# Moving weight loads in a fused attention and gated-FFN kernel: two gate/up pieces ahead of two stores, the down weights' loads retied, 40 instead of 64 rows in an opening load

## The chip, the cores and the metric

The kernel runs on one core of a Trainium2 chip. The metric is the device time of one execution in microseconds (us); lower is better. The core has TensorE (PE in the profile; its weight loads are PEld), VectorE (DVE), ScalarE (ACT), GpSimd (POOL) and SyncE (SP), which run in parallel and wait for each other by semaphores. [...]

## The reference

One transformer layer over x of 2048 rows by 640, in bf16. First a layer norm, then attention in 64 segments of 32 rows with a recurrent memory of 8 rows, then a residual, a second layer norm and a gated FFN, and a residual again.

```python
def _A_ref(x, mem0, Wq, Wk, Wv, Wo, seg_len):     # 32 heads of 128
    mem = mem0
    for s in range(n_seg):                         # 64 segments of 32 rows
        h = concat([mem, x[:, 32*s:32*s+32]])      # 40 rows
        q, k, v = h@Wq, h@Wk, h@Wv
        o = softmax(mask(q@k.T * Dh**-0.5)) @ v @ Wo
        mem = o[:, :8]                             # next segment's memory
        outs.append(o[:, 8:])

def _B_ref(x, W_gate, W_up, W_down):               # 640 -> 1728 -> 640
    return (relu(x @ W_gate) * (x @ W_up)) @ W_down

h  = x + _A_ref(_layernorm(x), ...)
h2 = h + _B_ref(_layernorm(h), ...)
```

A segment needs the memory that the segment before it made, so the 64 segments run one after the other.

## The kernel before

**How the order is made.** The program is a list of operations, each with an engine, the keys it reads and the keys it writes (`add`, `dma`, L348). `solve` (L46) puts a wait where a key was last written or read on another engine or by a DMA. Every engine executes its own operations in the order of the list. So the place of a `dma` call among the others decides its place in SP's queue, and nothing else: SP doesn't compute. While an SP operation waits, all that stands behind it on SP waits too.

**Opening (L746 to L793).** Nothing is in the chip's memory yet. SP issues the loads of Wk, Wq and Wv (15 loads of 1 MB) and of Wo (8 of 640 KB). ACT's queue loads 128 rows of x into `xt` (rows 0 to 63, then the last 64 rows of x), 128 rows into `x0` and the first memory. `row_stats`, `row_scale`, `ln1_trans` and `ln1_back` with b < 0 (L437 to L468) normalize and transpose `xt` and put it where the projections read it: the first 24 rows of each of segments 0 and 1 to `act_r`, the last 8 rows of segments 0, 1, 62 and 63 to `act_e`. Those last 8 rows are projected in groups of four segments. The first 24 rows of segments 62 and 63 aren't taken from this load.

**Segments (loop at L1026).** Each segment projects its rows, forms scores, probabilities, values and the output projection. Attention output rows go to a buffer in device memory, `attn_d`. The FFN is cut into four blocks of 512 rows, b = 0 to 3. As the attention ends, its weights' places are free one by one, and FFN weights are loaded into them: gate and up (Wg, Wu) where Wq was, down (Wd) where Wk was. The keys ("Wdone", j) say that all projections with Wq (0), Wk (1) or Wv (2) are through.

**FFN pieces.** The 1728 gate and up columns are 13 chunks j of 128 and a tail of 64. A pair is gate and up of one chunk (`gate_up`, L914): ten matmuls, a relu on ACT, a product on DVE into `hT`. Block 0's chunks 0 to 2 were computed during the last segments and come back from device memory into `hT` (the load from `hx_d`, L1300). Pair p of block 0 is chunk j = 3 + p. The pairs p = 0 to 3 run in the last segment's gaps; their matmuls have the line L832. From p = 4 on the line is L928, and the tail's is L941. Gate and up weights arrive in pieces (`load_piece`, L817), each with a key after which it may be issued: after the last VM load of segment 63, after the product of chunk NE (3), and so on. VM are copies of the attention values that `pv_x` (L692) reads.

**Down weights.** `load_down(n, p)` (L1260) loads chunks 3n to 3n + 2 of Wd, once Wk is free and the product of chunk 3 + p is there; n = 4 loads chunk 12 and the two halves of the tail. `down_pair` (L1235) multiplies; its first `down_part` (L1195) takes chunks 0 to 11 and so waits for Wd loads 0 to 3 at once. Its matmuls have the lines L1204 and L384.

**Rows and the second layer norm.** `rows` (L1270) projects the outputs of the last two segments: matmuls (L663), a copy on ACT and a sum on DVE (L1274) into `xt` or `xl`, then two stores of 24 rows to `attn_d`. For block 1, `ln2_load` (L731) loads x rows and attention rows, `ln2_front` (L736) adds them (L724) and normalizes on DVE and ACT, and `ln2_back` transposes them by DMA (L372). `h_rows` is block 0's residual, loaded from `h_d`; `down_out` (L1223, a DVE sum at L1226) adds it and `down_store` writes the result.

The order of SP's queue in the tail, as the list has it before the change: the VM loads, the two stores of segment 62's rows, two Wg pieces (chunks 7 to 10), a Wu piece, x and attention rows, a Wu piece, Wg and Wu for chunks 11 and 12, the load from hx, two stores of segment 63's rows, x and attention rows, two stores of late rows, four small loads of the gate/up tail (Wt), x and attention rows, Wd 0, x and attention rows, Wd 1, 2 and 3, h, Wd 4 with the tail, and the DMA transposes with the last gate and up pieces.

Of the kernel before, what the change touches and what calls it, by code (L numbers as in the profile page):

```python
# [177 lines left out]
def build_kernel(nc, A_x, A_mem0, A_Wq, A_Wk, A_Wv, A_Wo, A_seg_len, B_W_gate, B_W_up, B_W_down, out):  # L178
    _, S, D = A_x.shape
    M = A_mem0.shape[1]  # L180
    _, H, Dh = A_Wq.shape
    SEG = int(A_seg_len)
# [10 lines left out]
    RID = SEG - M  # L193
# [3 lines left out]
    x_ap, out_ap, mem0_ap = A_x[0], out[0], A_mem0[0]  # L197
# [4 lines left out]
    NE = 3  # L202
# [29 lines left out]
    hT = [ffn.alloc(f"hT{i}", [128, FC, TB], BF16) for i in range(2)]  # L232
# [6 lines left out]
    act_r = [ar.alloc(f"act_r{i}", [128, 4, DC, 32], BF16) for i in range(2)]  # L239
    act_e = [ar.alloc(f"act_e{i}", [128, DC, 32], BF16) for i in range(2)]  # L240
# [10 lines left out]
    VM = [ar.alloc(f"VM{i}", [128, 8, VW], BF16) for i in range(2)]  # L251
# [13 lines left out]
    xt = ar.alloc("xt", [128, D], BF16)  # L265
# [8 lines left out]
    def bank(b):  # L274
        return ps[:, b * 512:(b + 1) * 512]

    def bank_bf(b):
        return ps[:, b * 512:(b + 1) * 512].bitcast(BF16)
# [16 lines left out]
    def B(n):  # L295
        return ("B", n)
# [8 lines left out]
    for i in range(2):  # L305
        add("pool", lambda p, i=i: p.memset(act_r[i][:], 0.0),
            w=[("act", i, j, "m") for j in range(4)] + [("act", i, "x")] + [("act", i, "x", j) for j in range(4)])
# [6 lines left out]
    for g in range(4):  # L314
        for j in range(4):
            for r in range(2):
                sl, n = mca[32 * g:32 * g + 32, j, r, :], 0 if r == g % 2 else 1 + j
# [30 lines left out]
    def dma(dst, src, r=(), w=(), eng="sp"):  # L348
        add(eng, lambda e: e.dma_start(dst, src), r=r, w=w, dma=True)  # L349
# [12 lines left out]
    def row_stats(src, skey, n, more=()):  # L362
        row_moments(src, skey, n, more)
        row_std(n)

    def row_scale(src, skey, n, dst, dkey, eng="dve"):
        add(eng, lambda v: v.tensor_scalar(dst[0:n, :], src[0:n, :], mv[0:n, 0:1], rs[0:n, 0:1], ALU.subtract,
                                             ALU.mult), r=[skey, ("mv",), ("rs",)], w=[dkey])
# [5 lines left out]
    def transpose_rows(src, skey, n, b):  # L374
        def f(pe):
            for c in range(DC):
                i = pe.matmul(bank_bf(b)[:, c * 128:c * 128 + n], src[0:n, c * 128:(c + 1) * 128], ident[0:n, 0:n],
                              is_transpose=True)
            return i
        add("pe", f, r=[skey, ("ident",)], w=[B(b)])  # L380
# [56 lines left out]
            add("dve", lambda v: v.tensor_copy(dst, src), r=r, w=w)  # L437

    def n_rows(b):
        return 128 if b < 0 else min(128, S - 64 - 128 * b)  # L440

    def ln1_load(b, buf, key, eng="sp"):
        t0, n = 64 + 128 * b, n_rows(b)
        dma(buf[0:n, :], x_ap[t0:t0 + n, :], w=[key], eng=eng)

    def ln1_trans(b, buf, key, bk):
        transpose_rows(buf, key, 128 if b < 0 else min(128, S - 64 - 128 * b), bk)

    def ln1_back(b, src, r, eng):

        n = n_rows(b)

        def copy(dst, sl, w):
            if eng == "pool":
                add("pool", lambda p: p.tensor_copy(dst, sl), r=r, w=w)
            else:
                add("dve", lambda v: v.tensor_copy(dst, sl), r=r, w=w)
        if b < 0:
            for e in range(2):
                copy(act_r[1][:, e, :, M:32], src[:, :, SEG * e:SEG * e + RID], [("act", 1, "x", e)])  # L460
            copy(act_e[1][:, :, :].rearrange("p c (e t) -> p c e t", t=M),
                 src[:, :, :].rearrange("p c (e t) -> p c e t", t=SEG)[:, :, :, RID:SEG], [("acte", 1)])
            return
        for j in range(n // SEG):
            k = place(4 * b + 2 + j)[1]
            copy(act_r[b % 2][:, k, :, M:32], src[:, :, SEG * j:SEG * j + RID], [("act", b % 2, "x", k)])
        for j in range(n // SEG if n == 128 else 0):
            copy(act_e[b % 2][:, :, M * j:M * j + M], src[:, :, SEG * j + RID:SEG * j + SEG], [("acte", b % 2)])  # L468
# [277 lines left out]


    x0 = oTe[:].rearrange("p h t -> p (h t)")[:, 0:D]
    for n, t0 in enumerate((0, S - 64)):
        dma(xt[64 * n:64 * n + 64, :], x_ap[t0:t0 + 64, :], w=[("xt", "late") if n else ("xt",)], eng="act")  # L750
    ln1_load(0, x0, ("oTe", 0), "act")

    def mem_load(g, eng):
# [13 lines left out]
            A_Wo[16 * i + 4 * lo:16 * i + 4 * hi].rearrange("(g c) (p f) d -> (c p) g (f d)", c=4, f=4), w=[("Wo", i, lo)])  # L767
    ln1_load(1, xl, ("xl",))

    row_stats(xt, ("xt",), 128, [("xt", "late")])  # L770
    row_scale(xt, ("xt",), 128, xt, ("xt",))
    ln1_trans(-1, xt, ("xt",), P0)
    ln1_back(-1, chunks_of(bank_bf(P0)[:, 0:D]), [B(P0)], "dve")
    row_stats(x0, ("oTe", 0), 128)
# [13 lines left out]
    for j in (1, 0):  # L788
# [3 lines left out]
        for n, bks in enumerate(OB[j]):  # L792
            for i in range(2):  # L793
                t = 2 * (n % 2) + i
# [22 lines left out]
    def load_piece(key, eng="sp"):  # L817
        t, n, src, g, lo, hi = pieces.pop(0)
        a, b = GROUPS[g]
        dma(t[:, lo:hi, a:b], src[128 * lo:128 * hi, a:b].rearrange("(c p) f -> p c f", p=128), r=[("Wdone", 0), key],  # L820
            w=[(("Wg", "Wu")[n], g, lo)], eng=eng)
# [204 lines left out]
    for s in range(1, NSEG):  # L1026
# [16 lines left out]
        if s > 0:  # L1043
            a, ks = pass_act(s)
# [3 lines left out]
            elif s == NSEG - 3:  # L1048
                for n in range(2):
                    dma(ends[:, 1024 * n:1024 * n + 1024], ends_d[:, 1024 * n:1024 * n + 1024], r=[("ends",)],  # L1050
                        w=END_KEYS[2 * n:2 * n + 2])
# [32 lines left out]
            if s == NSEG - 2:  # L1084
                for n, (lo, hi) in enumerate(((0, 1), (1, 2), (2, 3), (3, DC))):
                    dma(xn2T[0][:, lo:hi, :], xn2_d[:, lo:hi, :], r=[("xn2_d", u) for u in range(4)] + [("Wdone", 0)],
                        w=[("xn2", 0, n)])
# [65 lines left out]
        if s == NSEG - 2:  # L1153
            p = 1 - place(s + 1)[0]
            add("pool", lambda o, p=p: o.tensor_copy(Qo[:, :, M:32], Qe[p][:, :, M:32]), r=[("Qe", p, i) for i in range(2)],
                w=[("Qo", i) for i in range(2)])
# [30 lines left out]
        if s == NSEG - 4:  # L1187
            p, j = place(NSEG - 1)
# [71 lines left out]
    def load_down(n, p):  # L1260
        lo, hi = 3 * n, min(3 * n + 3, FC - 1)
        r = [("Wdone", 1), ("hT", 0, NE + p)]
        dma(Wd[:, lo:hi, :], B_W_down[128 * lo:128 * hi, :].rearrange("(j p) d -> p j d", p=128), r=r, w=[("Wd", n)])
        if n == 4:
            for q in range(2):
                dma(Wd[FR * q:FR * q + FR, FC - 1, :], B_W_down[FM:F, :], r=r, w=[("Wd", 5 + q)])
# [3 lines left out]
    def rows(bk, p, s):  # L1270
        halves_pass(bk, oT[p], oT_keys(p, 0) + oT_keys(p, 1), range(16))
        tmp = bass.AP(at, 0, [[D, 64], [1, D]]).bitcast(F32)
        add("act", lambda a: a.activation(tmp, bank(bk)[64:128, 0:320], ACTF.Copy), r=[B(bk)], w=[("at",)])
        add("dve", lambda v: v.tensor_tensor(rowbuf(p), tmp,  # L1274
                                             bank(bk)[0:64, 0:320], ALU.add), r=[B(bk), ("at",)], w=[("wtok", p), (("xl",), ("xt",))[p]])
        for dg in range(2):
            dma(attn_d[32 * s:32 * s + RID, 2 * dg:2 * dg + 2, :].rearrange("t g f -> t (g f)"),
                bass.AP((xl, xt)[p], (32 * dg + M) * D, [[D, RID], [1, 320]]), r=[("wtok", p)],
                w=[("attn", 32 * s, g) for g in (2 * dg, 2 * dg + 1)])

    def rowbuf(p):
        return bass.AP((xl, xt)[p], 0, [[D, 64], [1, 320]])

    rows(P3, s % 2, s - 1)
    gate_up(0, NE + 1)
    load_piece(("VM", 0, 3))
    load_piece(("hT", 0, NE))
    pv_x(s, P0)
    norm_x(P0)
    norm_x_late(P0)  # L1290
# [8 lines left out]
    load_piece(("hT", 0, NE + 3))  # L1299
    dma(hT[0][:, 0:NE, :], hx_d[:, :, :], r=[("Wdone", 2), ("hT", 0, NE + 3)] + [("hx", n) for n in range(NE)],  # L1300
        w=[("hT", 0, n) for n in range(NE)])
    rows(P2, (s + 1) % 2, s)
    ln2_load(5)
    woe_pass(P3, range(16))
# [3 lines left out]
    for b in range(NBLK):  # L1308
        if 0 < b < NBLK - 1:
            for u in range(4):  # L1310
                ln2_load(4 * (b + 1) + u)
        for j in range(FC):
            p = j - NE if b == 0 else j
            if b or p > 3:
                gate_up(b, j)
            if b == 0 and p == 4:
                for q, src in enumerate((B_W_gate, B_W_up)):
                    for e in range(2):
                        r0 = FR * (q ^ e)
                        dma(Wt[:, e, :, r0:r0 + FR], src[:, FM:F].rearrange("(c p) f -> p c f", p=128),  # L1320
                            r=[("Wdone", 0), ("hT", 0, j)], w=[("Wt", q, e)])
            if b == 0 and p in (4, 5):
                ln2_load(p + 2)
            if b == 0 and 4 <= p < 8:
                for n in ((0,), (1, 2), (3,), (4,))[p - 4]:
                    load_down(n, p)
            if b == 0 and p == 6:
                dma(h_rows[0][:, :, :], h_d[:, :].rearrange("(u p) d -> p u d", p=128), r=[("h_d", u) for u in range(4)] +
                    [("Wdone", 1), ("hT", 0, j)], w=[("h", 0, u) for u in range(4)])
            if b == 0 and p in (8, 9):  # L1330
                load_piece(("hT", 0, j))
                load_piece(("hT", 0, j))
            if b + 1 < NBLK:
                fronts, backs = ((4, 6), (7, 9)) if b == 0 else ((1, 3, 5, 7), (3, 5, 7, 9))
                if p in fronts:
                    ln2_front(4 * (b + 1) + fronts.index(p))
                if p in backs:
                    ln2_back(4 * (b + 1) + backs.index(p), None)
        if b == 0:
            for u in (6, 7):  # L1340
                ln2_front(u)
                ln2_back(u, None)
        assert not pieces
        for n in range(2):
            down_pair(b, n)
# [63 lines left out]
```

## Time and profile before

| | |
|---|---|
| median of 3 runs | 998.86 us (998.84 to 999.37) |
| the profiled execution | 997.24 us |
| its span in the profile | 995.5 us |
| TensorE busy | 967.0 us (97%) |
| VectorE, ScalarE, GpSimd busy | 711.4, 521.4, 167.0 us |
| granted TensorE clock | 1.0 |
| opening, until the last Wv load is there | 0 to 41 us |
| tail of block 0 (from pair 0 to the end of its down projection) | 811 to 858.6 us |

The profile shows one execution of its own; its time is 997.24 us, 1.74 us more than its span, and 1.62 us less than the median of the runs shown. A busy TensorE isn't TensorE at its peak: matmuls are pipelined and their ends are modelled. The chain that ended last is followed back from the last instruction; what stands in it sets the end, and idle time of an engine outside it costs nothing. In a timeline row the first number is the start in us from the span's start, the second the duration, then engine, line, operation and tiles; the brackets say how long the engine stood idle before, and what released it. "SPq" is SP's queue: its rows say when a load was issued, not when it landed.

### The profile page before, as it was taken

What the parts mean: (1) busy time and instruction counts of PE and PEld (TensorE: products, weight loads), DVE (VectorE), ACT (ScalarE), POOL (GpSimd) and SP (SyncE); (2) the same over time, 40 slices, a digit from 0 to 9 for tenths busy, and PEclk for the clock granted to TensorE, in tenths of its full rate; (3) what the DMA queues carried; (4) which work ended last, traced back from release to release, by engine and by line L of the source; (5) the groups of instructions that cost most, each with busy time, mean ns of one, the idle gap of its engine ahead of it and who ended that gap; (6) DMA issues with size and microseconds to landing.
All of it is one profiled execution on the core that took longest, in us unless ns stands there. A gap on an engine that the chain in (4) does not pass through costs nothing.

```text
span 995.5 us, 56301 instructions
## 1 busy us (share of the span) xinstructions
PE 967.0 (97%) x26077; PEld 530.9 (53%) x24848; DVE 711.4 (71%) x1856; ACT 521.4 (52%) x1324; POOL 167.0 (17%) x412
## 2 busy tenths in 40 slices
PE   4799999999999999999999999999999999999998
PEld 1145555556555555555555655556565564444443
DVE  2468787878887887888788878787877865445332
ACT  1356666666666666666666666656665552122120
POOL 7011202021312130213022202021210010000000
PEclk9999999999999999999999999999999999999999
DMA  9941212121222122212312131112123259613100
GB/s 364 418 146 36 51 32 54 28 54 50 59 45 54 48 54 42 54 52 51 46 49 54 48 55 41 44 46 41 40 62 79 78 148 262 146 20 96 24 14 27
DMA packets 79135, 77.43 MB, mean 78 GB/s; under 512 B 45328, under 2 KB 64816, under 8 KB 76976
## 3 DMA queue, kind: packets, MB, share of 16 engines
q1 hardware_dynamic: 77136, 72.84, 26.6%
q8 instruction: 200, 3.28, 1.4%
q10 hardware_dynamic: 1760, 0.99, 0.4%
q14 instruction: 39, 0.32, 0.1%
HBM read 39.94 MB, written 7.74 MB: 48 GB/s over the span
## 4 chain that ended last, share of the span: by engine, by line
PE 93%; DMA 3%; DVE 1%; SPq 1%; issue 0%; ACT 0%; POOL 0%; DVEq 0%; ACTq 0%; POOLq 0%
PE ps L411 47%; PE ps L928 9%; PE ps L384 8%; PE ps L603 7%; PE ps L620 7%; PE ps L663 4%; PE ps L1204 3%; DMA W<-in_A_Wv_dram 3%; PE ps L504 2%; PE ps L692 2%; PE ps L557 2%; PE ps L832 2%; SPq L349 1%; DMA Wd<-in_B_W_down_dram 1%; PE ps L941 0%
## 5 line engine op out<-in xcount | busy, mean ns | idle before, releaser
L411 PE MATMUL ps<-W,act_r 128*32 128x512 bf16 (+1 forms) x8301 | 454.0, 358 | 1.2 <-DVE act_r L644 0.8
L411 PEld LDWEIGHTS ps<-W,act_r 128*32 128x32 bf16 x8301 | 212.7, 96 | 165.5 <-DVE act_r L644 31.5
L435 ACT ACTIVATE tok<-ps 128x512 bf16<-128x512 f32 x186 | 107.2, 594 | 56.7 <-PE ps L411 48.7
L411 PE MATMUL ps<-W,act_e 128*32 128x512 bf16 x1152 | 112.8, 382 | 6.5 <-DMA W<-in_A_Wv_dram 4.1
L430 DVE STREAM_TRANSPOSE Ko<-tox 128x512 bf16<-128x512 bf16 x128 | 89.6, 701 | 41.1 <-ACT tox L435 40.8
L435 ACT ACTIVATE tox<-ps 128x512 bf16<-128x512 f32 x134 | 79.6, 598 | 64.6 <-PE ps L411 45.0
L583 DVE STREAM_TRANSPOSE oT<-tox 128x512 bf16<-128x512 bf16 x128 | 94.9, 741 | 0.0
L430 DVE STREAM_TRANSPOSE Qo<-tok 128x512 bf16<-128x512 bf16 x124 | 85.3, 688 | 0.8
L603 PE MATMUL ps<-Wo,oT 128*32 128x160 bf16 x4032 | 81.6, 233 | 0.0
L620 PE MATMUL ps<-Wo,oT 128*32 128x320 bf16 x2016 | 79.8, 299 | 0.6 <-DVE rm L567 0.6
L384 PE MATMUL ps<-W,act_e 128*32 128x512 bf16 x808 | 79.8, 384 | 0.0
L603 PEld LDWEIGHTS ps<-Wo,oT 128*32 128x32 bf16 x4032 | 70.3, 97 | 11.2 <-DVE oT L577 3.1
L435 ACT ACTIVATE Vp<-ps 128x512 bf16<-128x512 f32 x127 | 75.2, 592 | 0.5 <-ACT Vp L435 0.5
L633 ACT ACTIVATE SA<-TA 64x40 f32<-64x40 f32 x126 | 29.5, 234 | 75.3 <-DVE TA L631 74.5
L956 ACT ACTIVATE g<-ps 128x512 bf16<-128x512 f32 x49 | 28.4, 593 | 76.1 <-PE ps L928 74.6
L520 ACT ACTIVATE Pm<-ps 128x64 bf16<-128x64 f32 x126 | 28.1, 223 | 74.1 <-PE ps L504 74.0
L957 DVE TENSOR_TENSOR hT<-g,ps 128x512 bf16<-128x512 bf16 x49 | 33.5, 686 | 40.3 <-PE ps L928 35.8
L620 PEld LDWEIGHTS ps<-Wo,oT 128*32 128x32 bf16 x2016 | 52.8, 96 | 16.6 <-DVE rm L567 1.3
L504 PE MATMUL ps<-Qo,Ko 128*32 128x40 bf16 x2048 | 61.2, 181 | 0.0
L577 DVE STREAM_TRANSPOSE oT<-om 128x128 bf16<-128x128 bf16 x126 | 38.9, 309 | 31.1 <-ACT om L569 31.1
L504 PEld LDWEIGHTS ps<-Qo,Ko 128*32 128x32 bf16 x2048 | 46.3, 94 | 25.8 <-DVE Qo L430 18.4
L1204 PE MATMUL ps<-Wd,hT 128*128 128x320 bf16 (+4 forms) x225 | 57.9, 299 | 2.0 <-DMA Wd<-in_B_W_down_dram 2.0
(131 smaller groups left out, 1436.3 us busy)
## 6 DMA issues: line engine op xcount, KB each, us to landing
VM<-Vp SPq DMA_DIRECT2D x126, 65.0 KB
VM<-Vp SPq DMA_DIRECT2D x63, 130.0 KB
W<-in_A_Wk_dram SPq DMA_DIRECT2D x5, 1024.0 KB
W<-in_A_Wq_dram SPq DMA_DIRECT2D x5, 1024.0 KB
W<-in_A_Wv_dram SPq DMA_DIRECT2D x5, 1024.0 KB
Wo<-in_A_Wo_dram SPq DMA_DIRECT2D x8, 640.0 KB
attn_d<-wtok SPq DMA_DIRECT2D x248, 7.5 KB
xt<-in_A_x_dram SPq DMA_DIRECT2D x16, 160.0 KB
```

Source lines behind the costliest of these rows:

```text
L384: return pe.add_instruction(mybir.InstMatmult(name=nc.get_next_instruction_name(), engine=mybir.EngineType.PE, ins=[pe.lower_ap(rhs), pe.l ...
L411: ins = pe.matmul(*b, start=(c == ends[0]), stop=(c == ends[1]), skip_group_check=True)
L430: add("dve", lambda v: v.transpose(dst[:, 16 * i:16 * i + 16, 0:32], tok[t][:, :].rearrange("p (h f) -> p h f", f=32)), r=tok_keys(t), w=keys)
L435: add("act", lambda a: a.activation(dst, src, ACTF.Copy), r=r, w=w)
L504: i = pe.matmul(bank((P0, P1)[hf])[q:q + 32, o:o + 40], (Ko if a == 0 else Ke[p])[:, h, :], Qo[:, h, :], start=True, stop=True, skip_group ...
L577: add("dve", lambda v: v.transpose(ap(oT[par], 160 * hf, [[40, 4], [320, 4], [1, 8]]), ap(om, 128 * hf, [[1, 4], [4, 32]])), r=[("om", hf) ...
L583: add("dve", lambda v, kh=kh: v.transpose(ap(oT[p], 160 * kh + M, [[320, 4], [40, 4], [1, 32]]), ap(tox, 128 * kh, [[256, 4], [1, 4], [4, ...
L603: i = pe.matmul(bank(bk)[32 * gg:32 * gg + 32, 0:160], src[:, hb, 0:32], w[:, gg], start=(hb == CH[16 * halves[0]]), stop=(hb == CH[-1]), ...
L620: i = pe.matmul(bank(bk)[32 * q:32 * q + 32, 0:320], src[:, hb, 0:32], w, start=(n == 0), stop=(n == 7), skip_group_check=True)
L663: ins = pe.matmul(bank(bk)[32 * q:32 * q + 32, 0:320], src[:, hb, 0:32], w[:, 2 * (q % 2):2 * (q % 2) + 2], start=(i == 0), stop=(i == 15) ...
L928: ins = pe.matmul(bank(bk), w[:, c, lo:lo + 128], xn2T[par][:, c, :], start=(c == 0), stop=(c == DC - 1))
L1204: i = pe.matmul(*a, start=(j == 0), stop=(j == FC - 1), skip_group_check=True)
```

## The change

Three edits.

1. The two `load_piece` calls for Wg's chunks 7 to 10 move ahead of `rows(P3, ...)`, so ahead of the two stores of segment 62's rows in SP's queue. Their keys stay the same.
2. Wd loads 0 and 1 are issued right after the load from `hx_d`, with the key of pair 3 in place of pairs 4 and 5. Load 2 goes to pair 4, load 3 to pair 5 and load 4 (with the tail) to pair 6, each in the place where Wd loads stood. Load 4 now comes before the load of h, which is at pair 6 too. The bytes are the same.
3. In the opening, only the last 40 rows of x are loaded into the second part of `xt` in place of 64: the last 8 rows of segment 62 and all of segment 63. Statistics, scaling and transposes work on 104 rows. The three copies to `act_r` and `act_e` become one of both segments' 24 rows (240 elements a partition) and two of 16 rows (80 elements).

```diff
-        return 128 if b < 0 else min(128, S - 64 - 128 * b)
+        return HEAD if b < 0 else min(128, S - 64 - 128 * b)
+    HEAD = 64 + SEG + M
...
         if b < 0:
-            for e in range(2):
-                copy(act_r[1][:, e, :, M:32], src[:, :, SEG * e:SEG * e + RID], [("act", 1, "x", e)])
-            copy(act_e[1][:, :, :].rearrange("p c (e t) -> p c e t", t=M),
-                 src[:, :, :].rearrange("p c (e t) -> p c e t", t=SEG)[:, :, :, RID:SEG], [("acte", 1)])
+            copy(act_r[1][:, 0:2, :, M:32], src[:, :, 0:2 * SEG].rearrange("p c (e t) -> p e c t", t=SEG)[:, :, :, 0:RID],
+                 [("act", 1, "x", e) for e in range(2)])
+            for e, t0 in ((0, RID), (2, 2 * SEG)):
+                copy(act_e[1][:, :, M * e:M * e + 2 * M].rearrange("p c (e t) -> p c e t", t=M),
+                     src[:, :, t0:t0 + SEG + M].rearrange("p c (a t) -> p c a t", t=M)[:, :, 0::SEG // M, :], [("acte", 1)])
...
-    for n, t0 in enumerate((0, S - 64)):
-        dma(xt[64 * n:64 * n + 64, :], x_ap[t0:t0 + 64, :], w=[("xt", "late") if n else ("xt",)], eng="act")
+    for p0, p1, t0, key in ((0, 64, 0, ("xt",)), (64, HEAD, S - HEAD + 64, ("xt", "late"))):
+        dma(xt[p0:p1, :], x_ap[t0:t0 + p1 - p0, :], w=[key], eng="act")
...
-    row_stats(xt, ("xt",), 128, [("xt", "late")])
-    row_scale(xt, ("xt",), 128, xt, ("xt",))
+    row_stats(xt, ("xt",), HEAD, [("xt", "late")])
+    row_scale(xt, ("xt",), HEAD, xt, ("xt",))
...
+    load_piece(("VM", 0, 3))
+    load_piece(("hT", 0, NE))
     rows(P3, s % 2, s - 1)
     gate_up(0, NE + 1)
-    load_piece(("VM", 0, 3))
-    load_piece(("hT", 0, NE))
     pv_x(s, P0)
...
     dma(hT[0][:, 0:NE, :], hx_d[:, :, :], ...)
+    load_down(0, 3)
+    load_down(1, 3)
     rows(P2, (s + 1) % 2, s)
...
-            if b == 0 and 4 <= p < 8:
-                for n in ((0,), (1, 2), (3,), (4,))[p - 4]:
-                    load_down(n, p)
+            if b == 0 and 4 <= p < 7:
+                load_down(p - 2, p)
```

More of the change, by code (lines that the diff above doesn't have):

```diff
@@ L446, in ln1_trans @@
     def ln1_trans(b, buf, key, bk):
-        transpose_rows(buf, key, 128 if b < 0 else min(128, S - 64 - 128 * b), bk)
+        transpose_rows(buf, key, HEAD if b < 0 else min(128, S - 64 - 128 * b), bk)
     def ln1_back(b, src, r, eng):
```

## The prediction

> **What bounds the kernel now.** I read the page first (busy time, the chain that ended last), then the chain in time order, then who waited for whom, the timeline at the places these named, and last the DMA view and the busy table by stretches.
>
> ```profile
> span 995.5 us, 56301 instructions
> PE 967.0 (97%) x26077; PEld 530.9 (53%) x24848; DVE 711.4 (71%) x1856; ACT 521.4 (52%) x1324; POOL 167.0 (17%) x412
> PE 93%; DMA 3%; DVE 1%; SPq 1%; issue 0%; ACT 0%; POOL 0%; DVEq 0%; ACTq 0%; POOLq 0%
> ```
>
> TensorE is the bound, and no edit here takes a matmul from it (the transposes of the opening shrink from 128 to 104 columns, under a DMA wait). A gain can only come out of the 3% of the chain that is DMA. In time order the chain has two such pieces:
>
> ```profile
> 13.47 27.55 DMA W<-in_A_Wv_dram
> ...
> 836.05 7.27 DMA Wd<-in_B_W_down_dram
> 843.33 0.09 issue
> ```
>
> The first is the opening, the second one stall in the tail; the waits between 795 and 860 us and the timeline size it:
>
> ```profile
> PE ps L1204 <- DMA Wd<-in_B_W_down_dram: 2.0, 1, 2.0
> SPq L349 <- DVE xl L1274: 1.4, 1, 1.4
> 840.15 1.25 PE L941 MATMUL ps<-xn2T,Wt 128*128 128x256 bf16 x10
> 843.42 0.30 PE L1204 MATMUL ps<-Wd,hT 128*128 128x320 bf16 x1 [2.01 <-DMA Wd<-in_B_W_down_dram]
> 834.48 0.48 DVE L724 TENSOR_TENSOR h<-xt,at 128x640 bf16<-128x640 bf16 x1
> ```
>
> TensorE ends the last gate/up work of block 0 and waits for the down weights. L941's ten matmuls are modelled as 1.25 us; the same amount of work in L928 starts every 1.08 us, so with nothing to wait for L1204 would start at 840.15 + 1.08 = 841.23. The stall is worth 843.42 - 841.23 = 2.19 us at most.
>
> Are the DMA engines full all the way to that stall? The busy table (last two columns: DMA share, GB/s):
>
> ```profile
> 816.00:819.00 3.00, 3.00 (x84) 1.54 (x80) 1.28 (x3) 1.03 (x2) 0.00 (x0) 1.00 0.12 21
> 819.00:828.00 9.00, 8.84 (x207) 5.50 (x197) 4.26 (x8) 2.68 (x6) 0.40 (x1) 1.00 0.97 300
> 828.00:832.00 4.00, 4.00 (x21) 1.81 (x19) 2.50 (x6) 0.75 (x2) 0.00 (x0) 1.00 0.48 119
> 836.00:844.00 8.00, 5.94 (x34) 3.03 (x31) 3.85 (x8) 2.86 (x7) 0.00 (x0) 1.00 1.05 365
> ```
>
> No: two holes, 3.00 x 0.88 = 2.6 us free before 819 and 4.00 x 0.52 = 2.1 us free in 828 to 832, and then a jam from 836 on in which Wd waits.
>
> **Counting SP's queue.** The DMA view from 800 us to a chosen time counts packets done on the queue. Here it is up to 816.0, 818.7, 831.3, 839.2, 839.3 and 841.9 us:
>
> ```profile
> q1 hardware_dynamic: 2473, 1.92, 43.1%
> q1 hardware_dynamic: 2545, 1.95, 37.5%
> q1 hardware_dynamic: 6065, 5.04, 55.2%
> q1 hardware_dynamic: 10051, 7.00, 63.0%
> q1 hardware_dynamic: 10083, 7.04, 63.2%
> q1 hardware_dynamic: 10859, 7.99, 65.7%
> ```
>
> The two 24-row stores of L349 issued at 817.06 added 72 packets: 24 rows and 12 completions each. So a load costs its contiguous runs plus one packet per ring it uses; by that rule everything issued before Wt comes to 6065, exactly what is done at 831.3. Going on (Wt 2624, x and attention rows 2 x 288, the four Wd loads of three chunks 4 x 400), the last load L1204 waits for is complete at packet 10,865. The count passes that at 841.9; the semaphore came at 843.33. The slowest ring thus trails by 1.4 us.
>
> **The change, part by part.**
>
> *Two gate/up pieces ahead of the stores.* SP now meets the first Wg piece right after the VM loads, and it waits for VM to land. The count stands still at 2473 from 816.0, so VM has landed then, and the pieces go out at about 816.0 instead of 817.82. Two issues (0.92 us) are over by 817.0; the two stores queued behind them wait for the row sum at 817.04 anyway (issued 817.06). Nothing behind them moves: the next, a Wu piece, waits for hT until 818.87. TensorE uses these pieces at 827.2, without a wait now: cost and direct gain 0. What moves is the DMA work: 672 packets fall into the empty 816 to 819. At 822.4 SP had issued 4177 packets and 3637 were done; that backlog of 540 (some 1.5 us at the 370 a microsecond of those rows) is gone, so the queue runs dry that much earlier before 828.
>
> *Wd.* Loads 0 and 1 leave 833.56 and 835.04 and go out behind hx at 824.75. On SP two issues cost 2 x 0.48 us, and SP sits there until 826.15 for DVE's xl sum (the 1.4 us above): hidden. On the rings they cost 800 packets / 290 a microsecond (the rate from 837.0 to 841.6) = 2.76 us. Free are 2.1 us plus the 1.5 us of the first edit: they fit. Taken out of the jam, L1204's loads are complete at packet 10,865 - 800 = 10,065, which is 839.25; with the same 1.4 us trail 840.6. TensorE wants them at 841.23: the stall goes with 0.6 us to spare. Ends: 0 (the loads are late after all) and -2.19. I take -2.15, near the upper end, for the wake-up after a semaphore (0.09 us in the chain) may not vanish whole.
>
> *What is late next.* Wd for chunk 12 and the tails (304 packets, now before h) is done 1.05 us after 839.25, with the trail 841.7; TensorE gets there 24 x 0.136 us after 841.23, at 844.5. h (528 packets) then lands by 843.6; DVE's first L1226 needs it at 851.06 - 2.15 = 848.9. The first DMA transpose moves up past nothing it needs. The last transpose hangs on DVE (L367 ends 848.99), which doesn't move; the DMA engines are idle from 855 to 860, so it has landed before 855, and block 1's first matmul wants it at 858.5 - 2.15 = 856.4. From there to the end TensorE has no DMA wait, so the gain stays.
>
> *What is queued behind loads 0 and 1:* the xl stores (nobody reads them before the last block), and x and attention rows for L724 at 834.48. Without any help from the first edit their packets are done 800 later, (5993 + 800 - 5543) / 290 after 827.36 = 831.7, plus the trail 833.1. With help earlier. No cost.
>
> *Opening, 40 rows for 64.* 24 rows x 1280 B = 30.7 KB less at the 426 GB/s of the full slices: -0.07 us if the bytes of all rings count, 0 if the fullest ring does. The 24-row stores used 12 rings, not 16, so 40 rows need not spread evenly; I take -0.03. [...] The copies of VectorE change from 2 x 0.175 + 0.23 = 0.58 us to one of 240 and two of 80 elements, the second waiting for the first: between 0.5 and 0.75 us by the rows for 120 to 160 and for 40 elements (0.20 each with a wait). At most 0.17 us late at 10.7 us: TensorE waits 0.23 us for Wq at 28.63, and 27.55 us of the chain are the Wv load. 0.
>
> **Sum.** -2.15 - 0.03 = -2.18 us. Profiled execution: 997.24 (span 995.5 and 1.74 around it) becomes 995.06. The median of the runs shown is 998.86, 1.62 above it: 996.68.
>
> **Rivals.**
>
> *SP is held.* The load of attention rows at 827.36 took 1.54 us to issue, a like one 0.43. In the opening SP was held whenever about 1,357 packets were outstanding (2208 issued, 850 done at 18.24; 3360 and 2004 at 38.24). With 800 more at 825.7 the count would be 6433 - 4900 = 1,530 without the first edit's 540, about 1,000 with them. If one slow ring is what holds SP, a hold of 2.8 us more puts the Wt loads and the last two Wd issues at up to 837.4 instead of 835.04; behind one and a half loads fewer they land at 842.0 to 842.6. A stall of 0.8 to 1.4 stays: 997.5 to 998.1, say 997.8.
>
> *No change.* Another semaphore of L1204 came with Wd. Against it: hx was done by 828, hT 11 by 838.9. 998.8.
>
> *Slower.* The rows for L724 are late. VectorE works in order: behind L724 stand the products of pair j=10, behind its statistics on ScalarE the relu of j=10, which frees the bank that TensorE takes for j=12 at 838.0; relu j=10 ended 837.19, so 0.8 us are spare. It decides when the rows land after 835.3; from there each microsecond is one on TensorE, and slower than before it gets after 837.5. With both the hold above (2.8) and two trails (2.8) behind 833.1 they land at 838.7: +3.4 - 2.19 = +1.2, 1000.1.
>
> **How the numbers follow.** Stall gone: 0.73, own range 996.4 to 997.0. SP held: 0.12. No change: 0.05. Rows late: 0.10. A measurement tells about 0.2%, 2.0 us, from no change: 996.86 is the bound, just beside my number, so a quarter of the first case falls within it: faster 0.55, within 0.38 (0.18 + 0.12 + 0.05 + 0.03), slower 0.07. The range reaches from 996.1 (full stall, the opening's 0.07 and 0.5 of spread between runs) to 998.9, which leaves out the slower case and little else.
>
> **What the new profile would show.** Right: no idle before L1204, starting near 841.2; Wd issued twice at 824.8; the DMA share of 816 to 819 and 828 to 832 up, Wg at 816; the chain without a Wd piece; an opening whose Wv piece ends at 41.0. Wrong: idle before L1204 with Wd as releaser and SP's issues of 827 to 836 stretched; or idle before L724 with a hole on TensorE at 838.

## The result and the profile after

The changed kernel takes 995.96 us (995.25 to 996.75, 9 runs) against 998.76 us (996.86 to 1000.2, 9 runs) of the kernel before on the same chip: ratio 0.9975, 95% interval 0.9964 to 0.9985, some 2.5 us less. The forecast was 996.7 in a range of 996.1 to 998.9, counted from a median of 998.86. The 995.96 lies 0.14 us below that range; the measured ratio on 998.86 gives 996.4, which lies in it.

The profile tells another story than the times do. The profiled execution of the changed kernel took 996.75 us against 997.24 of the one before, which is 0.5 us apart, not 2.5. The lines that matter here have moved by 3: L928 is L931, L941 is L944, L1204 is L1207.

The page of the changed kernel, with busy time and the shares of the chain:

```profile
span 995.0 us, 56316 instructions
PE 968.9 (97%) x26093; PEld 530.3 (53%) x24848; DVE 711.5 (72%) x1856; ACT 521.7 (52%) x1324; POOL 167.6 (17%) x412
PE 94%; DMA 3%; DVE 1%; SPq 1%; issue 0%; ACT 0%; POOL 0%; DVEq 0%; ACTq 0%; POOLq 0%
```

The timeline of TensorE around the place of the stall, with the idle time before an instruction in brackets:

```profile
838.92 1.24 PE L931 MATMUL ps<-xn2T,Wu 128*128 128x512 bf16 x5
840.00 1.26 PE L944 MATMUL ps<-xn2T,Wt 128*128 128x256 bf16 x10
842.93 0.30 PE L1207 MATMUL ps<-Wd,hT 128*128 128x320 bf16 x1 [1.68 <-DVE hT L954]
```

By the measure of the prediction (1.08 us behind the start of L944) L1207 could start at 841.08. It starts at 842.93: a stall of 1.85 us is left of 2.19. The brackets no longer name Wd, and the chain has no Wd piece either, but goes through the last product of the tail. Its pieces in order of time:

```profile
827.11 13.06 PE ps L931 x60
840.16 1.11 PE ps L944 x10
...
841.29 0.39 ACT g L951
...
841.77 0.43 DVE hT L954
842.20 0.73 issue
842.93 0.30 PE ps L1207
```

That is a wrong name for the same wait. The product of L954 is chunk 13, which L1207 does not read in its first part, and the 0.73 us of "issue" behind it have no cause there. The last product that it does read, chunk 11, is done at 838.7. The last experiment below settles it: there L1207 starts before L954 does. What was late is again Wd, as SP's queue shows (start, duration of the issue). First the rows of the kernel before:

```profile
830.33 1.01 SPq L349 DMA_DIRECT2D Wt<-in_B_W_gate_dram  x2
831.38 1.10 SPq L349 DMA_DIRECT2D Wt<-in_B_W_up_dram  x2
...
835.04 1.50 SPq L349 DMA_DIRECT2D Wd<-in_B_W_down_dram  x3
```

And those of the changed kernel:

```profile
816.79 0.92 SPq L349 DMA_DIRECT2D Wg<-in_B_W_gate_dram  x2
817.76 2.30 SPq L349 DMA_DIRECT2D attn_d<-xt  x2
...
824.81 1.03 SPq L349 DMA_DIRECT2D Wd<-in_B_W_down_dram  x2
...
830.12 1.78 SPq L349 DMA_DIRECT2D Wt<-in_B_W_gate_dram  x2
831.94 2.30 SPq L349 DMA_DIRECT2D Wt<-in_B_W_up_dram  x2
834.28 0.52 SPq L349 DMA_DIRECT2D xt<-in_A_x_dram  x1
834.85 0.43 SPq L349 DMA_DIRECT2D at<-attn_d  x1
835.32 0.43 SPq L349 DMA_DIRECT2D Wd<-in_B_W_down_dram  x1
835.80 0.49 SPq L349 DMA_DIRECT2D xt<-in_A_x_dram  x1
836.33 0.43 SPq L349 DMA_DIRECT2D at<-attn_d  x1
836.80 2.28 SPq L349 DMA_DIRECT2D Wd<-in_B_W_down_dram  x4
```

Loads 0 and 1 of Wd go out at 824.8, as meant. But the four small Wt loads now take 1.78 and 2.30 us to issue; before, they took 1.01 and 1.10. From 834.28 on SP issues without a pause, so the last load that L1207 needs, Wd 3, goes out at 836.80. Its new place in the queue had the time 835.04 before. In the kernel before, Wd 3 was the third of the loads in the row at 835.04 and went out at 836.05, so it now goes out 0.75 us later than before, not earlier; what is better is that loads 0 and 1 are no longer just ahead of it. The DMA view gives the packets done on this queue from 800 us up to 831.9, 839.2 and 841.2:

```profile
q1 hardware_dynamic: 6854, 5.89, 61.7%
q1 hardware_dynamic: 10306, 7.34, 64.8%
q1 hardware_dynamic: 10830, 7.97, 66.3%
```

At 831.9 SP had issued 6065 + 800 + 1312 = 8,177 packets, so 1,323 were outstanding. That is near the count that the prediction read in the opening (about 1,357), but the count alone doesn't hold SP. With these 1,323 outstanding the third of the four Wt loads went out at 831.94 in 0.53 us, and only the fourth took 1.73 us. In the kernel before, SP had 6065 + 1968 = 8,033 issued and 6537 done at 831.95, so 1,496 outstanding, and the fourth load, issued from then on, took 0.53 us. That SP is slow on these loads is measured; what holds it stays open. The prediction had 10,865 packets done at 839.25; at 839.2 it was 10,306. The count passes 10,865 at 841.3, and with the trail of 1.4 us behind it that gives 842.7, just ahead of L1207's start.

The busy table by stretches (the last two columns are DMA share and GB/s):

```profile
816.00:819.00 3.00, 3.00 (x81) 1.30 (x76) 1.42 (x4) 0.65 (x2) 0.00 (x0) 1.00 0.31 73
819.00:828.00 9.00, 9.00 (x205) 5.51 (x198) 4.28 (x8) 2.69 (x6) 0.40 (x1) 1.00 0.90 267
828.00:832.00 4.00, 4.00 (x20) 1.78 (x19) 2.35 (x6) 0.89 (x2) 0.00 (x0) 1.00 1.02 358
832.00:836.00 4.00, 4.00 (x20) 1.86 (x19) 3.25 (x7) 1.22 (x3) 0.00 (x0) 1.00 0.68 133
836.00:844.00 8.00, 6.32 (x38) 3.13 (x32) 4.00 (x9) 2.83 (x7) 0.00 (x0) 1.00 0.97 298
```

In the kernel before, 832 to 836 read:

```profile
832.00:836.00 4.00, 4.00 (x20) 1.81 (x19) 3.19 (x7) 1.36 (x4) 0.00 (x0) 1.00 0.91 180
```

The hole in 828 to 832 is filled (0.48 before, 1.02 now). But a new one has opened in 832 to 836 (0.91 before, 0.68 now): with SP behind, the DMA engines ran out of work there (a share of 0.17 from 834 to 834.5, just as SP comes free). Of the 800 packets brought forward only 255 were gained by 839.2 (10,306 against 10,051).

So two questions stand. Which of the three edits makes the difference? And why is the difference in time larger than what the stall lost?

### The profile page after: what moved, and what is told of

It is laid out like the page before. It is cut to its first block, busy times and chain, and to the rows that moved or that the text cites. A ratio compares the mean times of both kernels' runs of the same rounds, so it can differ in the third digit from the quotient of the medians.

```text
span 995.0 us, 56316 instructions
## 1 busy us (share of the span) xinstructions
PE 968.9 (97%) x26093; PEld 530.3 (53%) x24848; DVE 711.5 (72%) x1856; ACT 521.7 (52%) x1324; POOL 167.6 (17%) x412
## 4 chain that ended last, share of the span: by engine, by line
PE 94%; DMA 3%; DVE 1%; SPq 1%; issue 0%; ACT 0%; POOL 0%; DVEq 0%; ACTq 0%; POOLq 0%
PE ps L411 47%; PE ps L931 10%; PE ps L384 8%; PE ps L606 7%; PE ps L623 7%; PE ps L666 4%; PE ps L1207 3%; DMA W<-in_A_Wv_dram 3%; PE ps L507 2%; PE ps L695 2%; PE ps L560 2%; PE ps L835 2%; SPq L349 1%; PE ps L944 0%; PE ps L1220 0%
## 5 line engine op out<-in xcount | busy, mean ns | idle before, releaser
L1207 PE MATMUL ps<-Wd,hT 128*128 128x320 bf16 (+4 forms) x225 | 57.9, 299 | 1.7 <-DVE hT L954 1.7
```

The costliest lines, as they stand in the source:

```text
L1207: i = pe.matmul(*a, start=(j == 0), stop=(j == FC - 1), skip_group_check=True)
```

## The experiments

**Each edit alone.** The first run is the kernel before itself, unchanged, as a gauge for what counts as a difference.

> The kernel before, unchanged, to see how much its stall ahead of the down projection varies from one profiled execution to the next. Theory A (the gain is the Wd stall of 2.19 us): TensorE again stands idle some 2.0 us before L1204, between 1.5 and 3. Theory B (the stall varies by more than 1 us between executions, so that one profile doesn't size it): an idle time outside 1.5 to 2.5. Ratio 1.000 to the kernel before in both.

It took 997.55 us, ratio 0.9998 (0.9989 to 1.0007). The first edit alone:

```diff
+    load_piece(("VM", 0, 3))
+    load_piece(("hT", 0, NE))
     rows(P3, s % 2, s - 1)
     gate_up(0, NE + 1)
-    load_piece(("VM", 0, 3))
-    load_piece(("hT", 0, NE))
```

> Only the two gate/up pieces ahead of the stores of segment 62's rows. Prediction: no time by itself; 1.5 us of DMA work move from after 819 to before it, and the queue runs dry earlier before 828, but the Wd loads are issued no earlier, so the stall stays near 2.0 us: -0.0 to -0.3 us, ratio 0.9997 to 1.000. Rival (the first store behind the pieces holds SP for 1.9 us, as in the profile of the changed kernel, and delays the next Wu piece to 820.1): 0 to +0.5 us, and the queue is as late as before at 828.

997.76 us, ratio 0.9998 (0.9988 to 1.0008): no difference, within an interval of about 1 us either way. The second edit alone:

```diff
+    load_down(0, 3)
+    load_down(1, 3)
     rows(P2, (s + 1) % 2, s)
...
-            if b == 0 and 4 <= p < 8:
-                for n in ((0,), (1, 2), (3,), (4,))[p - 4]:
-                    load_down(n, p)
+            if b == 0 and 4 <= p < 7:
+                load_down(p - 2, p)
```

> Only the Wd loads retied (0 and 1 behind hx, 2, 3, 4 at pairs 4, 5, 6). Prediction: by packets 800 leave the jam and 2.1 us of free DMA time take most of them: the four loads land at 840.6 to 841.4 and the stall falls from 2.2 to 0.0 to 0.2 us: -2.0 us, ratio 0.998. Rival (SP is held at about 1,357 outstanding packets, so that the Wt loads and the last Wd issues slip by 2 us): Wd 3 issued near 837, a stall of 1 to 1.8 us stays: -0.4 to -1.2 us, ratio 0.9988 to 0.9996.

995.95 us, ratio 0.9979 (0.9969 to 0.9989): the effect of the whole change. Its timeline:

```profile
840.29 1.25 PE L941 MATMUL ps<-xn2T,Wt 128*128 128x256 bf16 x10
842.39 0.30 PE L1204 MATMUL ps<-Wd,hT 128*128 128x320 bf16 x1 [0.84 <-issue]
```

A stall of 1.02 us is left, where the expectation had at most 0.2. The Wt issues take 0.96 and 1.86 us, 0.7 more in all than in the kernel before, where the changed kernel lost 2.0; Wd 3 goes out at 835.84. The third edit alone (`HEAD`, 104 rows, in place of 128, and the three copies):

```diff
-    for n, t0 in enumerate((0, S - 64)):
-        dma(xt[64 * n:64 * n + 64, :], x_ap[t0:t0 + 64, :], w=[("xt", "late") if n else ("xt",)], eng="act")
+    for p0, p1, t0, key in ((0, 64, 0, ("xt",)), (64, HEAD, S - HEAD + 64, ("xt", "late"))):
+        dma(xt[p0:p1, :], x_ap[t0:t0 + p1 - p0, :], w=[key], eng="act")
```

> Only the 40 rows in place of 64 in the opening. Prediction: 0 to -0.1 us, the last Wv load lands at 41.0 us as before. Rival (the opening carries part of the measured 2.8 us, which the tail in the profile of the changed kernel doesn't show): -0.5 to -1.5 us, with the last Wv load before 40.5 us or fewer waits behind it.

997.58 us, ratio 1.0003 (0.9993 to 1.0013): again no difference. So the Wd edit alone carries the gain.

These runs brought up something else. In all three profiles without the Wd edit, the stall was longer than the 2.19 us of the first profile: 3.40 (kernel before again), 2.72 (first edit), 2.54 (third edit). The first of them has an idle of 3.22 us, outside 1.5 to 2.5, so one profile doesn't size this stall (theory B of the first expectation). And in two of them the granted clock fell behind it. The kernel before again, in single microseconds (the clock is the third column from the right):

```profile
843.00:844.00 1.00, 0.00 (x0) 0.00 (x0) 0.97 (x3) 0.00 (x0) 0.00 (x0) 1.00 1.06 390
844.00:845.00 1.00, 0.83 (x6) 0.40 (x4) 0.70 (x3) 0.23 (x1) 0.00 (x0) 0.94 1.93 268
845.00:846.00 1.00, 1.00 (x6) 0.28 (x2) 0.60 (x2) 0.27 (x2) 0.00 (x0) 0.50 1.47 125
846.00:847.00 1.00, 1.00 (x6) 0.23 (x3) 0.96 (x3) 0.00 (x0) 0.00 (x0) 0.50 0.47 109
847.00:848.00 1.00, 1.00 (x5) 0.24 (x2) 0.38 (x2) 0.50 (x2) 0.00 (x0) 0.50 1.09 308
848.00:849.00 1.00, 1.00 (x8) 0.38 (x4) 0.45 (x1) 0.00 (x0) 0.00 (x0) 0.85 1.12 330
```

Half speed for about 3.4 us, 1.7 us of work lost. From L1204's start to block 1's first matmul it takes 16.76 us here, and 15.1 where the clock stays up. With an idle of 3.22 us (this run) and 2.55 us (first edit alone, 16.48 us) the clock fell; with 2.37 us (third edit) and 2.01 us (the first profile) it did not. That made a second theory: a stall costs its own length (theory A), or that and, when it is long, a half-speed stretch behind it (theory C).

**Filling the stall with matmuls.** The kernel before, with eight additional 128x512 matmuls into a bank whose content is overwritten, between the tail's gate/up and the down projection:

```diff
+        if b == 0:
+            warm(8)
         for n in range(2):
             down_pair(b, n)
```

> The kernel before, with eight extra 128x512 matmuls (0.216 us each, 1.73 us) behind the gate/up tail of block 0, into a bank that the down projection starts anew; their result is overwritten. They fill part of the wait for Wd and leave it as long as it was. Theory C (a wait of some 2.5 us and more also drops the granted clock to 0.5 for some 3 us, which costs 1.4 to 1.7 us on top): Wd lands as before, L1204 starts 2.2 to 3.4 us after 841, but the idle time is under 1.7 us, the clock stays 1.0 between 844 and 850, and the median falls by the share of executions that had the drop, 0.5 to 1.2 us, with a shorter upper tail: ratio 0.9988 to 0.9995. Theory A (only the length of the wait counts): ratio 1.000.

997.46 us (one of 11 runs above 998.44) against 998.09 (11 of 27 above 998.44): ratio 0.9993 (0.9984 to 1.0002). In its profile the stall is 2.80 us from the end of L941's work, only 0.89 us of it idle, and the granted clock stays at 1.00. The additional work costs no time that shows. Fewer runs lie high, but the bound of 998.44 was taken from these runs themselves and the interval includes 1, so a larger effect was wanted. For that, Wd 3 was tied to the seventh pair, so that the stall is long in every execution, without and with twelve such matmuls:

```diff
-                for n in ((0,), (1, 2), (3,), (4,))[p - 4]:
+                for n in ((0,), (1, 2), (), (3, 4))[p - 4]:
```

> The kernel before, with the Wd load of chunks 9 to 11 tied to the seventh pair instead of the sixth, so that it goes out behind h (528 packets, 1.8 us at 290 a microsecond). Both theories: the stall before L1204 grows from the 2.2 to 3.4 us seen so far to 4.0 to 5.2 us. Theory A (a stall costs its own length): L1204's start to block 1's start stays at 15.1 us with the granted clock at 1.0, and the time is that of before plus about 1.8 to 2.2 us. Theory C (an idle of more than 2.5 us halves the clock behind it): the clock reads 0.5 for some 3 us behind L1204's start, 15.1 becomes 16.5 to 16.9, in every execution rather than in some, and the time is that of before plus 2.5 to 3.3 us.

> The same late Wd load, and 12 additional matmuls of 128 x 512 on bank 6 in the stall (about 2.8 us of work that needs no Wd; their product is overwritten). Theory A: the stall ends at the same moment, so the time is that of the late load without them, within 0.3 us. Theory C: the idle before L1204 is below 2.5 us, the clock stays at 1.0, and the time is 1.4 to 1.7 us below that of the late load without them.

1001.26 us (1000.7 to 1001.77) without, 999.09 us (998.64 to 999.57) with the matmuls: 2.17 us apart, with no overlap. The timeline of the run without them:

```profile
840.01 1.25 PE L941 MATMUL ps<-xn2T,Wt 128*128 128x256 bf16 x10
845.70 0.30 PE L1204 MATMUL ps<-Wd,hT 128*128 128x320 bf16 x1 [4.44 <-DMA Wd<-in_B_W_down_dram]
```

And with them:

```profile
839.81 1.25 PE L941 MATMUL ps<-xn2T,Wt 128*128 128x256 bf16 x10
840.90 2.75 PE L1272 MATMUL ps<-xn2T,Wt 128*128 128x512 bf16 x12
845.14 0.30 PE L1204 MATMUL ps<-Wd,hT 128*128 128x320 bf16 x1 [1.48 <-DVE mv L355]
```

The microsecond from 847 to 848, soon after the stall, first without and then with them (the granted clock is the third column from the right):

```profile
847.00:848.00 1.00, 1.00 (x5) 0.30 (x2) 0.69 (x3) 0.24 (x1) 0.00 (x0) 0.50 1.10 324
847.00:848.00 1.00, 1.00 (x10) 0.30 (x5) 0.49 (x2) 0.40 (x2) 0.00 (x0) 1.00 1.10 327
```

The stall is about as long in both, 4.61 and 4.25 us from the end of L941's work. (The releaser named in the second is the nearest event, not the cause.) Behind the long idle the clock is at 0.50 for about 3.4 us; behind the short one it stays at 1.00. From L1204's start to block 1 it takes 16.76 us without and 15.08 with. So 1.68 us of the 2.17 are the clock and 0.36 the shorter stall. Theory A, which said equal times within 0.3 us, falls; theory C holds, with the stall and the clock's price as it expected and the difference of the times somewhat above its 1.4 to 1.7.

**What holds SP.** With the Wd edit the stall shrinks but stays in the profiles. If SP is held at the Wt loads, then taking them off SP's queue, or sending Wd earlier, must end it. First the changed kernel with the four Wt loads on ScalarE's queue, beside the changed kernel itself:

```diff
-                            r=[("Wdone", 0), ("hT", 0, j)], w=[("Wt", q, e)])
+                            r=[("Wdone", 0), ("hT", 0, j)], w=[("Wt", q, e)], eng="act")
```

> The changed kernel with the four small Wt loads issued by ScalarE's queue in place of SP's. If SP's hold behind the Wt loads makes Wd 3 late: SP issues Wd 3 about 1.5 to 2 us earlier (near 835), the stall falls from 1.85 to under 0.5 us, another 1 to 1.5 us gained: ratio 0.9960 to 0.9966. If the DMA engines' work is the limit (the Wt packets are the same): Wd 3 lands no earlier, ratio 0.9972 to 0.9978. ScalarE spends about 2 us on the issues ahead of the second layer norm's statistics and may delay them by 0.5 us, which TensorE has 0.8 us to spare for.

> The changed kernel again, for a second profile of its tail. Theory A (stall gone but for chance): start of L1207 within 0.3 us of the end of the gate/up tail. Theory C with SP held: a stall of 0.8 to 1.9 us is left, SP's last two Wt issues take over 1 us each, and the clock stays 1.0. Ratio 0.9975 in both.

995.58 us for the changed kernel (ratio 0.9975, 0.9966 to 0.9983; stall in its profile 2.06 us), 996.47 for this one (0.9984, 0.9976 to 0.9993). The stall before L1207 is gone, and another one has come; the expected 0.9960 to 0.9966 was missed. ScalarE's timeline:

```profile
830.34 0.97 ACTq L349 DMA_DIRECT2D Wt<-in_B_W_gate_dram  x2
831.34 2.57 ACTq L349 DMA_DIRECT2D Wt<-in_B_W_up_dram  x2
833.96 0.29 ACT L358 ACTIVATE lv<-mv,eps 128x1 f32<-128x1 f32 x1 [4.83 <-issue]
```

And TensorE's:

```profile
835.03 1.25 PE L931 MATMUL ps<-xn2T,Wg 128*128 128x512 bf16 x5 [1.14 <-ACT g L959]
...
841.52 1.26 PE L944 MATMUL ps<-xn2T,Wt 128*128 128x256 bf16 x10
842.61 0.30 PE L1207 MATMUL ps<-Wd,hT 128*128 128x320 bf16 x1
```

The slow issue moved with the loads: ScalarE, too, takes 2.57 us for the last pair. There it delays a relu that TensorE waits for (1.14 us). TensorE so reaches the down projection only at 842.61, and a start at that time doesn't by itself show that Wd came earlier. The packets do: without Wt, L1207's loads are complete at packet 10,865 - 2624 = 8,241, which SP's queue passes at 838.8, 840.2 with the trail, against 841.3 and 842.7 in the changed kernel. Wd 3 goes out at 835.80 here, 1 us earlier, and its packets no longer stand behind those of Wt on one queue; the run doesn't separate the two. The other way is to spread Wd over the earlier part, where the engines have room (a DMA share of 0.31 from 816 to 819). Wd 0 goes behind the first Wg piece, Wd 1 behind the next x and attention rows (`ln2_load(4)`), Wd 2 behind hx, Wd 3 to pair 4 and Wd 4 to pair 5:

```diff
+    load_down(0, 0)
     load_piece(("hT", 0, NE))
...
+    load_down(1, 1)
...
-    load_down(0, 3)
-    load_down(1, 3)
+    load_down(2, 3)
...
-            if b == 0 and 4 <= p < 7:
-                load_down(p - 2, p)
+            if b == 0 and 4 <= p < 6:
+                load_down(p - 1, p)
```

> The changed kernel with the Wd loads spread over the holes: 0 behind the first Wg piece at 816.8, 1 behind the x and attention rows at 821, 2 behind hx, 3 at pair 4, 4 at pair 5. If the time of L1204 hangs on the Wd loads alone: they are there by 838, no idle time before L1207, 1.0 to 1.8 us less than the changed kernel: ratio 0.9957 to 0.9965. Rival (the added work in 817 to 822 delays the Wu and Wg pieces or the rows of the second layer norm): a new wait on TensorE at 827 or 838, ratio at or above 0.9975.

995.31 us (5 runs), ratio 0.9968 (0.9955 to 0.998): just above the expected 0.9957 to 0.9965; no stall in the profile, but too near to the changed kernel's 995.58 to tell apart. So both were taken again side by side:

> The changed kernel with the Wd loads spread out (behind the first Wg piece, the fourth norm's weights, hx, pair 4, pair 5). Beside the changed kernel on the same chip: no idle before L1204's counterpart, and 0.2 to 1.0 us less than the changed kernel if the stall of 1.9 to 2.1 us left in the changed kernel's profiles is worth its length in part of the executions; no difference if only the clock mattered.

> The changed kernel itself, for comparison with the spread loads on the same chip: 0.9975 of before as in the two earlier sets, a stall of 1.8 to 2.1 us before L1204's counterpart and the clock at 1.0 behind it.

994.40 us (994.31 to 994.91, 6 runs) against 995.67 (994.99 to 996.83, 12 runs) of the changed kernel; against before 0.9962 (0.9947 to 0.9976) and 0.9976 (0.9967 to 0.9985). The intervals overlap, while in this set every run of the spread version lies below every run of the changed kernel. The two sets put it 0.3 and 1.3 us ahead, and it has the lowest median of all versions. TensorE in its second profile:

```profile
839.41 1.26 PE L944 MATMUL ps<-xn2T,Wt 128*128 128x256 bf16 x10
840.51 0.30 PE L1207 MATMUL ps<-Wd,hT 128*128 128x320 bf16 x1
```

There is no wait at all, though SP is slow on the Wt loads here too (1.60 us on the last pair): Wd 3 has gone out at 833.22. And VectorE there:

```profile
841.18 0.42 DVE L954 TENSOR_TENSOR hT<-g,ps 64x256 bf16<-64x256 bf16 x1 [0.88 <-ACT g L951]
```

The product of L954 comes 0.67 us after L1207 has started, so L1207 never waited for it: in the changed kernel the releaser was misnamed, and the wait was for Wd.

## Why the prediction was right, and where not

- **Total:** -2.18 forecast, about -2.5 measured (0.9975), 996.7 against 995.96. Right, but partly by luck: a stall was left that the prediction had put at nothing, and the stall that it started from was larger in the other profiles than the 2.19 us it had read. The two errors go opposite ways (below).
- **Wd, -2.15, "the stall goes with 0.6 us to spare":** right that this edit alone carries the gain (0.9979 alone, the other two 0.9998 and 1.0003). Wrong that the stall is gone in the profiles: 1.85, 2.06 and 2.10 us in the three of the changed kernel and 1.02 in the Wd edit alone. The step that failed is the packet count: 10,865 at 839.25 assumed that SP issues on time, and at 839.2 it was 10,306.
- **SP is held (rival 1, 0.12):** SP's slow issues came about at the place that the rival named, the Wt loads, and Wd 3 went out at 836.80 against "up to 837.4". Its reason, a hold at about 1,357 outstanding packets, is not borne out: at 1,496 outstanding the kernel before issued the next load in 0.53 us. Its stall of 0.8 to 1.4 us was too small, and its time of 997.8 too high; by the estimate below, because the stall that it starts from is mostly longer than the 2.19 us of the profile.
- **What the stall was worth.** 2.19 us was one execution. Over the four profiles without the Wd edit it was 2.19, 3.40, 2.72 and 2.54, mean 2.71, and in two of the four the clock's 1.68 and 1.40 us came on top. An estimate of a time with neither: the spread version 994.40; the late Wd load 1001.26 - 4.61 - 1.68 = 994.97; the same with matmuls 999.09 - 4.25 = 994.84; mean 994.7, all from one chip. (With the spread version's other median there, 995.31, the mean is 995.0.) The kernel before on that chip, 998.02, is 3.3 us above it, and 2.71 + (1.68 + 1.40) / 4 = 3.5 is about that. The changed kernel, 995.67, is 0.9 above. So by this estimate the change took 2.4 of 3.3 us. Its profiles show 1.9 to 2.1 us of stall, more than these 0.9, but they come from executions of 996.75, 997.41 and 996.54 us, each in the upper part of its own runs (medians 995.96, 995.58, 995.67), while the first profile of before was 1.5 us below its median. A check by single executions: each profiled time less its own stall and its own loss by the clock gives 994.3 to 995.5 us in all the runs but the one with Wt on ScalarE; the profiled times themselves range from 994.3 to 1001.2. So stall and clock explain most of the spread, and about 1 us of it comes from elsewhere and wasn't found.
- **Pieces, 0:** right in time. "Two issues are over by 817.0" was not: Wg went out at 816.79 though the packet count stands still from 816.3, and the two stores took until 820.06. A hold of some 1 us at one or another issue between 816 and 824 appears in many of these runs, with the first edit and without it, in changing places (the stores here, Wg at 822.20 with the first edit alone, Wg at 817.37 in the kernel before again). It did no harm: TensorE is busy for 9.00 of the 9 us from 819 to 828. Its cause stays open.
- **Opening, -0.03:** no difference in time (1.0003 alone), and too small a term for the profiles to size: Wv is there at 40.94 instead of 41.02, but between executions this moment varies from 40.87 to 41.42 with 64 rows and from 40.59 to 41.19 with 40 rows. No run shows whether the bytes of all rings or those of the fullest one count, between which the -0.03 was chosen. What shows is the packets: those of ScalarE's queue fall from 448 to 418 up to 60 us, 30 fewer, which are 24 rows and 6 small ones (all packets under 512 B go from 640 to 634). A ring of the prediction stands in the trace only as such a small packet with its semaphore update: the load of 40 rows has 10 of them, one of 64 rows 16, a store of 24 rows 12. The copies were busy for 0.70 us, 0.62 from the first start to the last end, and TensorE waited for none of them.
- **Rows for L724 late:** did not happen. It starts at 834.50 against 834.48.
- **Signs:** Wd twice at 824.8, the fuller 828 to 832 and the chain without Wd came as written, the last only because the releaser was misnamed; L1204's counterpart at 841.2 did not (842.93). The sign for the opposite case, "idle before L1204 with Wd as releaser", would have been missed by the letter, since the profile named another releaser.

## What to carry to other kernels

One profile samples one execution: a stall that ends with a DMA varies here by more than 1 us from run to run (2.19 to 3.40 us in the four profiles without the Wd edit), so size it by several profiles or by the spread of the times before you subtract it. An earlier place in the queue does not bring a load out earlier if its issuer is held ahead of it (Wd 3 went out at 836.80 in place of 836.05); look in the new profile at how long each issue behind it takes, and put the early load where the engines are idle rather than ahead of a burst of small ones (994.40 us with Wd spread out, 995.67 for the changed kernel beside it). A long wait of TensorE can cost more than its length (4.61 us and another 1.68 by the clock with the late Wd load), and where it can't be removed, matmuls whose result nobody reads kept the clock up here (1.00 against 0.50).

## What the runs showed of the hardware

- Ahead of the down projection, an idle of TensorE of 2.55 us and more (2.55, 3.22, 4.44) was followed by a granted clock of 0.50 for about 3.4 us, worth 1.4 to 1.7 us; idles of up to 2.37 us were not. The length of the idle can't be all that decides. With the first edit alone the clock fell at about 843.2, 2.0 us after the idle began and before L1204 started; yet the idle of 2.37 us in another run passed without a drop. In the other two cases it fell 3.9 and 4.8 us after the idle began, when L1204 was running again. What else decides was not tested, so these rows give no safe length.
- An issuing engine took much longer for the same loads in some executions: SP up to 3.68 us for two Wt loads (the third profile of the changed kernel) and ScalarE 2.57 us, against 1.10 us in the kernel before. The number of outstanding packets on its queue doesn't decide it alone: a single such load went out in 0.53 us with 1,323 and with 1,496 outstanding. While SP was held, nothing behind on its queue was issued (Wd 3 at 836.80).
